# A planner whose segments end at dependences, a model of the shared port, and an opening with other orders and engines

## The chip, the cores and the metric

The kernel runs on one core of one Trainium2 chip. The metric is the device time of one execution in microseconds (us). The kernel before took 988.6 us, the median of three runs (987.35 to 989.39). The core's engines are TensorE (PE, with its weight loads apart as PEld), VectorE (DVE), ScalarE (ACT), GpSimd (POOL) and SyncE (SP), which issues every DMA of this kernel. Each engine works through its own list of instructions in the order in which they were emitted. Where one needs what another has written, it waits on a semaphore.

## The reference

Eight batches of attention with eight heads of 64: 32 global queries see all 544 keys, and 512 local queries see the 32 global keys and the keys at most 32 positions away. The 4352 rows that come out go through an MLP of 512, 2048 and 512 columns.

```python
def attention(q_l, k_l, v_l, q_g, k_g, v_g):          # B, H, S, D = 8, 8, 512 (32 global), 64
    k_all = np.concatenate([k_g, k_l], axis=2); v_all = np.concatenate([v_g, v_l], axis=2)
    out_g = sm(scale * q_g @ k_all.T) @ v_all
    s_ll = np.where(np.abs(pos[:, None] - pos[None, :]) <= 32, scale * q_l @ k_l.T, -1e9)
    out_l = sm(np.concatenate([scale * q_l @ k_g.T, s_ll], -1)) @ v_all
    return np.concatenate([out_g, out_l], axis=2)
def mlp(x, w_in, w_out):                              # 4352 x 512, 512 x 2048, 2048 x 512
    h = x @ w_in
    g = np.where(h >= 1, h, np.where(h <= -1, 0, (h + 1) ** 2 / 4))
    return g @ w_out
```

The softmax `sm` subtracts the row's maximum and divides by the sum. The two weight matrices come as 64-bit floats.

## The kernel before

**What is computed where.** Every product runs on TensorE in 16-bit halves: a number is a high and a low part, and three products of parts stand for one. So every operand is prepared first. ACT casts the high part, and DVE or POOL subtracts it to get the low part. The weights come as pairs of 32-bit words. `decode` puts the words of one tile of 128 x 512 together (ACT takes the magnitude, DVE shifts the low word and joins the two), `signed` sets the sign, TensorE sums the magnitudes for a scale, and `halves` scales and splits the tile; its three letters say on which engines (first `e`: on TensorE, with a float32 product by `const_sid`). There are 16 tiles of w_in (steps Lw, wd, ws, wh: load, decode, scale, halves) and 16 of w_out (Lo, od, oh).

**Attention.** K, Q and V of a batch are loaded, scaled and split (steps L, sk/sq/sv, pk/pq/pv), and K and Q are transposed. Step aa takes two heads of 128 queries: scores in `ps_s`, minimum and mask on DVE into `tts_t` and `small_nb`, a small DVE addition on `small_nb`, two exponentials on ACT into `pf_pf`, the high part into `const_pb`, the low part by POOL, and the transposed weights in `pt_pt`. Step ab multiplies these by V into `ps_x`, and step ax divides (`xn_xn`), splits (`xn_xh`) and transposes into `xt_xt` by a DMA. In batch 0 `turn` (lines 562 to 571) makes the transposes with eight matmuls by `const_ident` into PSUM and an ACT copy; in the other batches SP issues a transposing DMA.

**The MLP.** A stage is 256 rows, half a batch. Step m (`moe1`) makes two tiles of the hidden layer from `xt_xt` in 24 matmuls into `ps_h` and applies the activation on ACT, DVE, DVE, ACT and POOL (`moe_t_r`, `hidden_g`); step o (`moe2`) multiplies by w_out into `ps_o`. Step m2.0 is the first of the third stage, the second batch's first, and needs step ax11, the last of that half batch. There are 16 stages and two for the global rows.

**What sets the order.** The kernel is traced once into a list of calls. `segments` (line 152) groups successive calls of one step on one engine into a Segment, whose calls stay together; a call that reads what the call before it wrote adds 100 ns to the Segment's price. `schedule` (line 204) replays the Segments: on each engine the ready one with the smallest `prio` goes next. `prio` comes from the numbers in `T` (a nominal time of every step), then from `deadlines`, which counts back from the end. `plan` (line 310) does both, keeps the better, and `build` emits the calls in that order, so the order on every engine is fixed. Loads are paced: one is issued when the fifth before it has landed.

Until about 250 us the core prepares the weights, the first two batches and runs the first two stages; that part is called the opening here.

## Time and profile before

| what | value |
|---|---|
| median of the runs | 988.6 us |
| the profiled execution's own time | 987.26 us |
| its span, first to last instruction | 985.5 us |
| mean granted clock of TensorE | 0.968 |
| PE busy | 904.5 us, 92% |
| DVE busy | 730.4 us, 74% |
| ACT busy | 601.0 us, 61% |
| POOL busy | 359.5 us, 36% |

All times of rows are microseconds from the start of the span. A busy PE is not PE at its peak, since its records overlap. An instruction's duration is that from its start to its end; where two on one engine stand closer than the first one's duration, they overlap. What an engine waited for is inferred from semaphores. All instructions of the kernel before carry line 1238 (loads 1240), since they are emitted there; they are told apart by tiles, with buffer numbers left out.

### The profile page before, as it was taken

To read this page: it belongs to the slowest core of one execution; us is meant where nothing else is said; L and a number is where in the kernel's file an instruction comes from. 1 tells how busy PE (TensorE), PEld (TensorE's weight loads), DVE (VectorE), ACT (ScalarE), POOL (GpSimd) and SP (SyncE) were. 2 spreads that over 40 slices of the span, in tenths; PEclk is the share of its full clock that TensorE was granted. 3 is DMA by queue.
4 is the path that set the end of the run, shared out by engine and by line. 5 is a ranking of instruction groups with operands and counts; after the bars stand their busy time and mean duration, and the time that the engine had idled before them with its cause. 6 is when DMAs were issued, how large, how long until landed. Compare 5 with 4: busy or idle time off the path is not lost.

```text
span 985.5 us, 24720 instructions
## 1 busy us (share of the span) xinstructions
PE 904.5 (92%) x9499; PEld 641.4 (65%) x9500; DVE 730.4 (74%) x1956; ACT 601.0 (61%) x1418; POOL 359.5 (36%) x383
## 2 busy tenths in 40 slices
...
GB/s 236 233 147 64 168 88 102 145 161 144 175 155 177 119 128 152 182 113 128 153 186 45 134 111 170 136 114 130 160 175 114 128 134 108 59 79 66 33 1 33
DMA packets 370102, 125.23 MB, mean 127 GB/s; under 512 B 346432, under 2 KB 355648, under 8 KB 369984
## 3 DMA queue, kind: packets, MB, share of 16 engines
...
## 4 chain that ended last, share of the span: by engine, by line
PE 71%; DVE 16%; DMA 5%; issue 3%; ACT 2%; POOL 1%; SPq 1%; DVEq 0%; POOLq 0%; ACTq 0%
PE ps_h_h L1238 32%; PE ps_o_o L1238 30%; PE ps_s_s L1238 5%; PE ps_x_x L1238 5%; DVE tmp_tmp L1238 2%; DVE weights_w L1238 2%; DVE tts_t L1238 1%; DVE nat_nat L1238 1%; DMA xt_xt<-xn_xh 1%; DMA weights_w<-in_moe_w_in_dram 1%; DVE batch_small_ms L1238 1%; DVE ps_h_h L1238 1%; SPq L1238 1%; DVE moe_t_r L1238 1%; DVE batch_small_q L1238 1%
## 5 line engine op out<-in xcount | busy, mean ns | idle before, releaser
L1238 PE MATMUL ps_h_h<-xt_xt,weights_w 128*128 128x256 f16 (+1 forms) x3456 | 383.3, 270 | 10.2 <-ACT pt_pt L1238 6.0
L1238 PE MATMUL ps_o_o<-weights_w,hidden_g 128*128 128x512 f16 x1632 | 376.6, 381 | 2.8 <-DVE xt_xt L1238 2.8
L1238 PEld LDWEIGHTS <-weights_w 128*128 128x128 f16 x3456 | 321.7, 99 | 61.5 <-issue 15.5
L1238 PEld LDWEIGHTS <-hidden_g 128*128 128x128 f16 x1744 | 161.5, 100 | 177.6 <-issue 12.1
L1238 POOL TENSOR_TENSOR hidden_g<-moe_t_r,hidden_g 128x512 f16<-128x512 f32 (+1 forms) x144 | 165.6, 1150 | 273.2 <-ACT hidden_g L1238 267.2
L1238 POOL TENSOR_TENSOR const_pb<-pf_pf,const_pb 128x384 f16<-128x384 f32 (+1 forms) x124 | 129.3, 1045 | 276.9 <-DVE const_pb L1238 195.8
L1238 ACT ACTIVATE moe_t_r<-ps_h_h,batch_small_ms 128x512 f32<-128x512 f32 (+1 forms) x144 | 107.9, 749 | 127.2 <-PE ps_h_h L1238 119.3
L1238 DVE SCALAR_TENSOR_TENSOR ps_h_h<-ps_h_h,batch_small_ms,moe_t_r 128x512 f32<-128x512 f32 (+1 forms) x144 | 104.2, 723 | 93.0 <-ACT moe_t_r L1238 92.9
L1238 ACT ACTIVATE pf_pf<-tts_t,small_nb 128x224 f32<-128x224 f32 (+1 forms) x256 | 117.3, 459 | 91.2 <-DVE small_nb L1238 77.1
L1238 DVE CUSTOM_DVE_ANT_0 tts_t<-ps_s_s,const_mask,batch_small_q 128x192 f32<-128x192 f32 (+1 forms) x256 | 100.2, 427 | 41.1 <-PE ps_s_s L1238 39.0
L1238 ACT CAST hidden_g<-moe_t_r 128x512 f16<-128x512 f32 (+1 forms) x144 | 84.7, 588 | 61.0 <-DVE moe_t_r L1238 60.6
L1238 DVE SCALAR_TENSOR_TENSOR moe_t_r<-moe_t_r,batch_small_ms,ps_h_h 128x512 f32<-128x512 f32 (+1 forms) x144 | 103.4, 718 | 5.5
L1238 ACT ACTIVATE junk_junk<-stage_st 128x512 f16<-128x512 f32 (+1 forms) x108 | 67.5, 625 | 25.5 <-DMA stage_st<-in_v_l_dram 8.7
L1238 PE MATMUL ps_s_s<-kt_kt,qt_qa 128*128 128x32 f16 (+2 forms) x704 | 69.8, 199 | 10.4 <-DVE small_nb L1238 5.6
L1238 PEld LDWEIGHTS <-pt_pt 128*128 128x128 f16 (+1 forms) x1536 | 61.8, 98 | 15.4 <-ACT pt_pt L1238 2.5
L1238 PE MATMUL ps_x_x<-v_v,pt_pt 128*128 128x64 f16 (+1 forms) x1536 | 67.7, 194 | 0.8 <-DVE moe_t_r L1238 0.5
L1238 PE MATMUL ps_s_s<-kt_kt,qt_qb 128*128 128x32 f16 (+2 forms) x704 | 65.9, 198 | 0.0
L1238 PEld LDWEIGHTS <-qt_qb 128*128 128x128 f16 x704 | 55.4, 98 | 16.1 <-issue 13.1
L1238 PEld LDWEIGHTS <-qt_qa 128*128 128x128 f16 x704 | 59.4, 98 | 5.1 <-issue 1.5
L1238 DVE CAST const_pb<-pf_pf 128x384 f16<-128x384 f32 (+1 forms) x112 | 47.7, 431 | 10.7 <-DMA pt_pt<-const_pb 6.6
L1238 ACT ACTIVATION_READ_ACCUMULATOR pf_pf<-tts_t,small_nb 128x1 f32 x256 | 47.8, 187 | 0.0
L1238 DVE TENSOR_SCALAR small_nb<-small_nb 128x2 f32<-128x2 f32 x128 | 35.4, 277 | 4.4
(165 smaller groups left out, 900.5 us busy)
## 6 DMA issues: line engine op xcount, KB each, us to landing
...
```

What stands on the lines that cost most here:

```text
L1238: getattr(getattr(tc.nc, engine), op)(*a, **k)
```

## The change

The planner changes in four places. A Segment on DVE or ACT now ends where the next call reads what the call before it wrote, and calls of other steps may stand between the two. `shares` says which calls of DVE and POOL use a port that the two have in common, and `schedule` runs such calls one after the other (`pair`). `plan` makes one pass with `deadlines` and adds a number per step from a table, `LATER` (316 entries, in us). The prices of some calls and transfers are others.

The choice of engine moves into strings in `T`, read by `of`: `turns` (batch 0's 16 `pt_pt` are now DMA transposes, its ten K and Q ones stay), `casts` and `subs` (high and low part of `const_pb`), `glow`, `lows`, `splits`, `shifts` (six of 32 on POOL), `mags` and `halves`. `decode` can also take the magnitude on POOL. `win_scale` joins eight one-column maxima into three wider ones. In `T` the first tiles of w_in are loaded ahead of K and Q, and V much later.

```diff
+def shares(engine, op, a, k, tiles):
+    if engine == "gpsimd":
+        return op != "memset"
+    if engine != "vector" or op in ("memset", "reciprocal", "tensor_reduce", "tensor_tensor_reduce"):
+        return False
...
+    held = [x for x in ins if is_ap(x) and not tiles.get(x.tensor.name, (0, 0, 1))[2]]
+    return len(held) > 1 or (op in ("tensor_scalar", "tensor_copy") and len(held) == 1 and free(held[0]) > 1)
...
-            if cur is None or cur.engine != engine or engine == "sync" or fresh & {tiles[nm][0] for nm in cur.new}:
+            near = [x.tensor.name for x in sides(*cur.calls[-1])[0]] if cur and cur.engine == engine in ("vector", "scalar") else []
+            if (cur is None or cur.engine != engine or engine == "sync" or fresh & {tiles[nm][0] for nm in cur.new}
+                    or any(x.tensor.name in near for x in ins)):
                 cur = Segment()
...
-            near = [x.tensor.name for x in sides(*cur.calls[-2])[0]] if len(cur.calls) > 1 else []
-            cur.t += t + (100.0 if engine in ("vector", "scalar") and any(x.tensor.name in near for x in ins) else 0.0)
+            cur.t += t
+            cur.parts.append((t, shares(engine, op, a, k, tiles)))
...
+                done, slow = now, SLOW if e == "tensor" and now < 2.0e5 else 1.0
+                for t, shared in g.parts:
+                    if shared:
+                        pair = done = max(pair - LEAD, done) + t
+                    else:
+                        done += t * slow
...
-    for n in range(PASSES):
-        order, taken, end = schedule(segs, tiles, hop, slack, landing, ahead)
...
+    if T["late"]:
+        deadlines(segs, [g.n for g in segs], hop, slack, landing)
+    for g in segs:
+        g.prio += LATER.get(g.step, 0.0) * (1.0e3 if T["late"] else 1.0)
+    order, taken, _ = schedule(segs, tiles, hop, slack, landing, ahead)
...
-            for c in (n - 1, n):
-                nc.vector.tensor_max(W["tmh"][:, c:c + 1], wt[:, n - 1:n], wt[:, n:n + 1])
+            nc.vector.tensor_max(W["tmh"][:, n - 1:n + 1], wt[:, n - 1:n].broadcast_to([P, 2]), wt[:, n:n + 1].broadcast_to([P, 2]))
...
-        (nc.vector.tensor_copy if b else nc.scalar.copy)(pb[:, 0, :, :w], pf[:, :, :w])
-        nc.gpsimd.tensor_tensor(pb[:, 1, :, :w], pf[:, :, :w], pb[:, 0, :, :w], op=ALU.subtract)
+        (nc.scalar.copy if of("casts", b, 4 * i + pr, 16, "v") == "a" else nc.vector.tensor_copy)(pb[:, 0, :, :w], pf[:, :, :w])
+        (nc.vector if of("subs", b, 4 * i + pr, 16, "p") == "v" else nc.gpsimd).tensor_tensor(pb[:, 1, :, :w], pf[:, :, :w], pb[:, 0, :, :w], op=ALU.subtract)
...
-        turn(b, pt.rearrange("p j u c k -> p (j u c) k"), pb.rearrange("p j u c -> p (j u c)"))
+        turn(of("turns", b, 10 + 4 * i + pr, 30, "d"), pt.rearrange("p j u c k -> p (j u c) k"), pb.rearrange("p j u c -> p (j u c)"))
...
-T = dict(att=1.25, s0=72.5, s1=139.1, s2=221.06, wd0=8.61, wds=3.39, wd8=36.0, wdt=2.27, wh=1.5, whs=2.09, od=58.0, ods=2.6,
+T = dict(late=1, lk0=4.19, lq0=1.76, lv0=30, sk=12, sq=14, adds="vvvvvv1vvvvvvvvvvvvvavvvvvvvvv1v",
+         subs="pppppppppppvvvpppppppvpvvpppppvp", glow="pppppppppppvpppv",
...
```

The first place is the end of the first half tile of attention, on DVE. Before, it read as follows (the last call of one w_in tile's decode, then ax00, then the scales ms00; `DVE_49` is DVE's own semaphore):

```order
L1238 SCALAR_TENSOR_TENSOR tmp_tmp_3_120<-tmp_tmp_3_120,weights_w12_0_77 128x512 [waits DVE_49,Activation_49]
L1238 SCALAR_TENSOR_TENSOR weights_w12_0_77<-weights_w12_0_77,tmp_tmp_3_120 128x512 [waits DVE_49]
L1238 TENSOR_SCALAR small_den_0_161<-small_sum_0_138 128x8
L1238 RECIPROCAL small_rc_0_162<-small_den_0_161 128x8 [waits DVE_49]
L1238 TENSOR_TENSOR xn_xn_0_163<-ps_x_x_0_155,small_rc_0_162 128x512 [waits DVE_49,PE_49]
L1238 TENSOR_SCALAR batch_small_ms_0_170<-const_tm_0_131,batch_small_sv_0_123 128x2
L1238 TENSOR_SCALAR batch_small_ms_0_170<-batch_small_ms_0_170 128x2 [waits DVE_49]
L1238 RECIPROCAL batch_small_ms_0_170<-batch_small_ms_0_170 128x2 [waits DVE_49]
L1238 TENSOR_SCALAR batch_small_ms_0_170<-batch_small_ms_0_170 128x2 [waits DVE_49] x2
L1238 TENSOR_TENSOR batch_small_ms_0_170<-batch_small_ms_0_170 128x2 [waits DVE_49]
L1238 TENSOR_SCALAR batch_small_ms_0_170<-batch_small_ms_0_170 128x2 [waits DVE_49]
L1238 SCALAR_TENSOR_TENSOR batch_small_ms_0_170<-const_wt_0_81,batch_small_sv_0_123,batch_small_ms_0_170 128x2
```

Now the same two steps stand between others, and a w_out tile's decode (`stage_st_1`) is spread among them:

```order
L1280 TENSOR_SCALAR small_den_0_162<-small_sum_0_130 128x8
L1280 TENSOR_SCALAR stage_st_1_92<-stage_st_1_92 128x512 [waits DMAHW6_49,DMAHW5_49]
L1280 RECIPROCAL small_rc_0_163<-small_den_0_162 128x8 [waits DVE_49]
L1280 TENSOR_SCALAR batch_small_q5_0_113<-batch_small_q5_0_113,batch_small_sk_0_107 128x3
L1280 SCALAR_TENSOR_TENSOR tmp_tmp_1_87<-tmp_tmp_1_87,stage_st_1_92 128x512 [waits DVE_49,Activation_49]
L1280 TENSOR_TENSOR xn_xn_0_164<-ps_x_x_0_160,small_rc_0_163 128x512 [waits DVE_49,PE_49]
L1280 TENSOR_SCALAR batch_small_q5_0_113<-batch_small_q5_0_113 128x3 [waits DVE_49]
L1280 SCALAR_TENSOR_TENSOR weights_w0_0_66<-stage_st_1_92,tmp_tmp_1_87 128x512 [waits DVE_49]
L1280 TENSOR_SCALAR batch_small_ms_0_171<-batch_small_ms_0_171 128x2
L1280 TENSOR_SCALAR batch_small_ms_0_171<-const_tm_0_101,batch_small_sv_0_148 128x2
L1280 TENSOR_TENSOR const_tm_0_101<-const_tm_0_101 128x4
L1280 TENSOR_TENSOR batch_small_ms_0_171<-batch_small_ms_0_171 128x2 [waits DVE_49]
```

In this piece no row reads what the row ahead of it wrote. Counted over DVE's instructions up to the last of ax11, 231 of 471 waited for the very instruction ahead of them before, and 30 of 462 do now; 74 more wait for the one two ahead, where three did.

The second place is DVE's start. Before, its first rows were K's scale (`small_amk`, from ACT's squares) and Q's:

```order
L1238 MEMSET const_ones_0_82 128x128
L1238 TENSOR_REDUCE small_amk_0_91<-small_amk_0_91 128x1
L1238 TENSOR_SCALAR small_asx_0_93<-small_amk_0_91 128x1
L1238 COPY small_amk_0_91<-ps_s_s_0_97 128x1
L1238 TENSOR_SCALAR small_amk_0_91<-small_amk_0_91 128x1 x2
L1238 TENSOR_SCALAR batch_small_sk_0_98<-small_amk_0_91 128x1
L1238 RECIPROCAL batch_small_sk_0_98<-batch_small_sk_0_98 128x1
```

Now the first rows decode w_in tiles whose low words POOL has shifted:

```order
L1280 MEMSET const_ones_0_83 128x128
L1280 SCALAR_TENSOR_TENSOR tmp_tmp_0_96<-tmp_tmp_0_96,weights_w2_0_68 128x512
L1280 SCALAR_TENSOR_TENSOR tmp_tmp_1_87<-tmp_tmp_1_87,weights_w0_0_66 128x512
L1280 SCALAR_TENSOR_TENSOR tmp_tmp_2_95<-tmp_tmp_2_95,weights_w1_0_67 128x512
L1280 TENSOR_SCALAR weights_w3_0_69<-weights_w3_0_69 128x512
L1280 SCALAR_TENSOR_TENSOR weights_w1_0_67<-weights_w1_0_67,tmp_tmp_2_95 128x512
L1280 SCALAR_TENSOR_TENSOR tmp_tmp_3_97<-tmp_tmp_3_97,weights_w3_0_69 128x512
```

Tiles 2, 0 and 1 come first, two of DVE's calls for each, and K's scale comes after the fourth tile.

The third place is SP's queue in the middle of the opening, where before it held w_out's loads, copies of V and Q, and the first transposes into `xt_xt`:

```order
L1240 DMA stage_st_1_86<-in_moe_w_out_dram 128x512 x2
L1240 DMA stage_st_3_116<-in_moe_w_out_dram 128x512
L1238 DMA v2_v2_0_127<-v_v_3_126 64x1024
L1238 DMA qt_qb_2_157<-qt_qa_2_156 64x1024
L1240 DMA stage_st_3_116<-in_moe_w_out_dram 128x512
L1238 DMA qt_qb_2_157<-qt_qa_2_156 64x1024
L1238 DMA v2_v2_1_133<-v_v_5_132 64x1024
L1238 DMA_TRANSPOSE xt_xt_0_89<-xn_xh_0_164 128x8x128
L1238 DMA qt_qb_0_106<-qt_qa_0_104 64x1024 x2
L1238 DMA qg_qgb_0_166<-qg_qga_0_165 64x256 x2
L1240 DMA stage_st4_0_87<-in_k_l_dram 32x8x64
L1238 DMA_TRANSPOSE xt_xt_0_89<-xn_xh_0_164 128x8x128
```

Now the first `pt_pt` transposes stand there:

```order
L1282 DMA stage_st_0_93<-in_moe_w_out_dram 128x512 x2
L1280 DMA_TRANSPOSE pt_pt_0_134<-const_pb0_0_61 128x8x128
L1280 DMA_TRANSPOSE pt_pt_1_138<-const_pb1_0_62 128x8x128
L1280 DMA_TRANSPOSE pt_pt_2_145<-hidden_g_0_132 128x8x128
L1280 DMA v2_v2_0_156<-v_v_1_153 32x1024
L1280 DMA v2_v2_1_158<-v_v_1_153 32x1024
L1280 DMA v_v_0_159<-v_v_1_153 32x1024
L1280 DMA_TRANSPOSE pt_pt_0_134<-hidden_g_1_133 128x8x128
L1280 DMA v2_v2_0_156<-v_v_3_155 64x1024
L1280 DMA v2_v2_1_158<-v_v_5_157 64x1024
L1282 DMA stage_st_3_126<-in_moe_w_out_dram 128x512 x2
L1280 DMA_TRANSPOSE pt_pt_1_138<-const_pb0_0_61 128x8x128
```

All 16 of them go through SP, between the loads of w_out.

## Rows read from the trace of the kernel before

**Rows 1.** Windows: stretch, length, then busy us (instructions) per engine, clock, DMA share, GB/s.
```profile
0.00:253.00 253.00, 179.10 (x1791) 121.25 (x1793) 209.52 (x547) 186.32 (x412) 102.61 (x125) 0.88 0.64 149
253.00:985.50 732.50, 725.39 (x7709) 520.14 (x7707) 520.89 (x1410) 414.73 (x1006) 256.88 (x258) 1.00 0.64 119
...
0.00:248.00 248.00, 176.87 (x1753) 119.12 (x1755) 206.10 (x532) 182.48 (x399) 100.50 (x122) 0.89 0.63 149
```

**Rows 2.** Timeline of all engines, 244 to 254: start, us, instruction.
```profile
246.10 0.60 ACT L1238 CAST xn_xh<-xn_xn 128x512 f16<-128x512 f32 x1
...
246.23 0.17 DVE L1238 TENSOR_SCALAR small_nb<-small_nb 128x2 f32<-128x2 f32 x1
...
247.34 0.68 DVE L1238 TENSOR_TENSOR xn_xh<-xn_xn,xn_xh 128x512 f16<-128x512 f32 x1
...
249.51 1.30 SPq L1238 DMA_TRANSPOSE xt_xt<-xn_xh  x1
...
251.56 2.63 SPq L1238 DMA_TRANSPOSE pt_pt<-const_pb  x2
...
252.86 1.35 PE L1238 MATMUL ps_h_h<-xt_xt,weights_w 128*128 128x256 f16 x6 [0.58 <-DMA xt_xt<-xn_xh]
```

**Rows 3.** Timeline of DVE, first 13 us.
```profile
11.95 0.16 DVE L1238 TENSOR_REDUCE small_amk<-small_amk 128x1 f32<-128x5 f32 x1 [10.88 <-ACT junk_junk L1238]
```

**Rows 4.** Timeline of ACT, first 13 us.
```profile
7.91 0.20 ACT L1238 ACTIVATE const_warm<-const_pgb 128x1 f32<-128x1 f16 x1 [5.83 <-POOL small_amg L1238]
```

**Rows 5.** Groups of POOL, 0 to 248: busy us, mean ns of one, idle before.
```profile
L1238 POOL TENSOR_SCALAR tmp_tmp<-weights_w,const_wo 128x512 f32<-128x512 f32 x8 | 5.7, 722 | 4.0 <-DVE const_wo L1238 3.8
```

**Rows 6.** Groups of DVE, 0 to 248, same columns.
```profile
L1238 DVE SCALAR_TENSOR_TENSOR weights_w<-weights_w,tmp_tmp 128x512 int32<-128x512 int32 x15 | 13.8, 920 | 0.5
...
L1238 DVE SCALAR_TENSOR_TENSOR tmp_tmp<-tmp_tmp,stage_st 128x512 int32<-128x512 int32 x16 | 12.6, 788 | 2.3 <-ACT tmp_tmp L1238 0.7
L1238 DVE SCALAR_TENSOR_TENSOR weights_w<-stage_st,tmp_tmp 128x512 int32<-128x512 int32 x16 | 12.5, 782 | 0.6
...
L1238 DVE TENSOR_SCALAR small_nb<-small_nb 128x2 f32<-128x2 f32 x30 | 8.5, 284 | 1.0
...
L1238 DVE TENSOR_TENSOR weights_w<-tmp_tmp,weights_w 128x512 f16<-128x512 f32 x5 | 4.1, 826 | 0.0
L1238 DVE TENSOR_SCALAR batch_small_ms<-batch_small_ms 128x2 f32<-128x2 f32 x10 | 4.0, 400 | 0.3
```

**Rows 7.** Timeline of DVE near 28 and 95.
```profile
28.04 0.15 DVE L1238 TENSOR_SCALAR small_w<-small_w 128x1 f32<-128x1 f32 x1
28.23 0.16 DVE L1238 RECIPROCAL small_w<-small_w 128x1 f32<-128x1 f32 x1
28.31 0.13 DVE L1238 TENSOR_SCALAR small_w<-small_w 128x1 f32<-128x1 f32 x1
...
94.83 1.46 DVE L1238 SCALAR_TENSOR_TENSOR tmp_tmp<-tmp_tmp,stage_st 128x512 int32<-128x512 int32 x1
...
97.47 0.69 DVE L1238 SCALAR_TENSOR_TENSOR tmp_tmp<-tmp_tmp,stage_st 128x512 int32<-128x512 int32 x1
98.19 0.69 DVE L1238 SCALAR_TENSOR_TENSOR weights_w<-stage_st,tmp_tmp 128x512 int32<-128x512 int32 x1
98.80 0.41 DVE L1238 CUSTOM_DVE_ANT_0 tts_t<-ps_s_s,const_mask,batch_small_q 128x192 f32<-128x192 f32 x1
```

**Rows 8.** Timeline of POOL near 93.
```profile
93.22 2.53 POOL L1238 TENSOR_TENSOR weights_w<-tmp_tmp,weights_w 128x512 f16<-128x512 f32 x2
```

**Rows 9.** Groups: the first batch's transposes on PE, and ACT's moves.
```profile
L1238 PE MATMUL ps_h_h<-const_ident,const_pb 128*128 128x128 f16 x96 | 8.6, 229 | 8.9 <-DVE moe_t_r L1238 3.4 <-POOL const_pb L1238 2.4 <-ACT const_pb L1238 1.2
...
L1238 ACT COPY pt_pt<-ps_h_h 128x1024 f16<-128x1024 f16 x16 | 16.0, 1002 | 0.3 <-PE ps_h_h L1238 0.2
```

**Rows 10.** Waits of PE, 0 to 250: engine, tile, releaser: us, times, longest.
```profile
PE ps_h_h L1238 <- ACT pt_pt L1238: 8.2, 7, 2.2
```

**Rows 11.** DMA issues, 0 to 250: count, median us from issue to landing.
```profile
pt_pt<-const_pb SPq DMA_TRANSPOSE x10, 3.3
```

More of the change, by code (lines that the diff above doesn't have):

```diff
@@ L129, in cost @@
         run = min(tuple(x.ap[-1])[1] * mybir.dt.size(x.dtype) for x in (o, ins[0]))
-        return 560.0, b / (186.0 if run < 512 else 264.0 if run < 1024 else 280.0)
+        return 560.0, b / (215.0 if run < 512 else 340.0)
     if engine == "scalar":
-        own = 90 if op != "activation" or mybir.dt.size(o.dtype) == 2 else 190 if "accum_out" in k else 235
+        ptr = any(free(x) == 1 for x in ins[1:])
+        if "accum_out" in k:
+            own = 190 if ptr else 95
+        elif mybir.dt.size(o.dtype) == 2:
+            own = 185 if ptr else 90
+        else:
+            own = 235 if ptr else 135
         return own + n / 1.2 + (93 if "accum_out" in k else 0), 0
@@ L148 @@
 class Segment:
-    __slots__ = ("n", "engine", "calls", "t", "xfer", "after", "before", "new", "uses", "load", "step", "left", "ready", "prio", "t0", "done")
+    __slots__ = ("n", "engine", "calls", "t", "xfer", "after", "before", "new", "uses", "load", "step", "parts", "left", "ready", "prio", "t0", "done")
 def segments(steps, tiles, prio, names):
@@ L221, in schedule @@
         if g.left == 0:
-            waiting[g.engine].append(g)
+            bisect.insort(waiting[g.engine], (g.prio, g.n, g))
     free_at = {e: 0.0 for e in engines}
-    dma_free, now, events, order, landed = 0.0, 0.0, [], [], []
+    dma_free, pair, now, events, order, landed = 0.0, 0.0, 0.0, [], [], []
     while len(order) < len(segs) or events:
@@ L232, in schedule @@
                 best = None
-                for g in waiting[e]:
-                    if g.ready > now or (best is not None and (g.prio, g.n) > (best.prio, best.n)):
+                for at, (_, _, g) in enumerate(waiting[e]):
+                    if g.ready > now:
                         continue
@@ L239, in schedule @@
                             need.setdefault(tiles[nm][0], []).append(place[nm])
-                    if any(len(slots[tag]) < len(x) + (min(x) > head[tag]) or max(x) - head[tag] >= many[tag] for tag, x in need.items()):
+                    if need and any(len(slots[tag]) < len(x) + (min(x) > head[tag]) or max(x) - head[tag] >= many[tag] for tag, x in need.items()):
                         continue
@@ L280, in schedule @@
                 c = segs[b]
-                wait = (hop if c.engine != g.engine else 60.0) + (slack if c.engine == "tensor" and g.engine != "tensor" else 0.0)
+                wait = (hop if c.engine != g.engine else OWN) + (slack if c.engine == "tensor" and g.engine != "tensor" else 0.0)
                 c.ready = max(c.ready, now + wait)
@@ L302, in deadlines @@
             c = segs[b]
-            wait = (hop if c.engine != g.engine else 60.0) + (slack if c.engine == "tensor" and g.engine != "tensor" else 0.0)
+            wait = (hop if c.engine != g.engine else OWN) + (slack if c.engine == "tensor" and g.engine != "tensor" else 0.0)
             x = min(x, late[b] - wait - took)
@@ L570, in turn, with of @@
             nc.tensor.transpose(t[:, c, :n], i[:, c * P:(c + 1) * P], ident[:n, :n])
-        nc.scalar.copy(o, t[:, :, :n])
+        (nc.scalar.copy if who == "a" else nc.vector.tensor_copy)(o, t[:, :, :n])
+    def of(what, b, n, most, other):
+        return T[what][most * b + n] if most * (b + 1) <= len(T[what]) else other
     def load_win(f):
@@ L630, in wout_decode @@
         raw = W.pop(("rawo", f))
-        m = decode(raw.rearrange("p c t -> p (c t)"), None, SHIFTS[NF + f])
+        m = decode(raw.rearrange("p c t -> p (c t)"), None, T["shifts"][NF + f], T["mags"][NF + f])
         mag = upper(m)
```

113 lines of the change are left out of this document (61 added, 52 removed), and 39 rows, old and new, of the table LATER.

## The prediction

> **What bounds the kernel now.** I read the windows first. From 253 us to the end PE is busy 725 of 732.5 us at a granted clock of 1.00, so that part is PE's own and ends when PE has done its matmuls. In the 253 us ahead of it PE is busy 179 us: some 74 us of PE are lost there, and almost nothing later [rows 1]. The cut is where the first matmul of the third stage, m2.0, starts, 252.9 us [rows 2]. So the time is the start of m2.0 plus what PE has left by then. Its work behind m2.0 is the same in both kernels to 0.3 us, by the sum of the matmuls' columns at 2.4 GHz that stand behind m2.0 in the two orders. The question is thus one number: when m2.0 can start.
>
> Then I followed m2.0 back in the timeline. It waits for the DMA transpose of `xn_xh`, which SP issued at 249.5, after DVE's subtraction of 247.3 to 248.0, the last call of ax11 on DVE [rows 2]. Up to there DVE is busy 206.1 of 248.0 us, ACT 182, PE 177 and POOL 100 [rows 1]; the engine that is nearest to full is DVE. Of its 41.9 idle us, 10.9 lie at the start, where its first real call waits for ACT's squares until 11.95 [rows 3]. The 31 that remain are many small pieces. So I treat the opening as DVE's, and forecast when DVE ends ax11.
>
> **The change part by part.** *The start.* DVE's first call is now the decode of w_in tile 2. It needs POOL's two shifts, which stand behind POOL's constants, and ACT's magnitude, which stands behind `const_warm`; that one starts at 7.91, as soon as POOL's memsets are through [rows 4]. Two POOL calls of 0.72 us by the nearest row [rows 5] after 7.9 it is about 9.4. DVE starts at 9.4 for 11.95: **-2.5 us**. The bounds are 0, if a load of w_in is late, and -3.5, if the shift is not waited for.
>
> *DVE's load.* Up to ax11 DVE has 462 calls for 471. Eight low parts (six of `const_pb`, two of `hidden_g`) come from POOL to DVE, at some 0.7 to 0.83 us by the nearest row, that of `weights_w` [rows 6]; six shifts, five column maxima, two casts and some single calls go. With each group's own mean, from the view whose dearest groups are [rows 6], that is 10.1 us less and 7.3 more: **-2.8 us**. The bounds are -4 (nine calls at the mean of 206.1/471) and +3 (nothing saved but the added low parts stretched).
>
> *Self-waits.* Of those calls 231 waited for the call right ahead, and 30 do now. The price of one such wait stands in the timeline: the second of two dependent calls starts 0.72 us after the first (97.47 to 98.19), an independent one of the same kind is followed after 0.61 (98.19 to 98.80); of small calls the dependent one starts after 0.19 (28.04 to 28.23), the independent one after 0.08 [rows 7]. Both differ by 0.11 us. So 201 fewer give **-22.1 us**. The cover is gone only where the call put between waits for another engine itself, since DVE takes its calls in order; bounded by 0 and -22. The 74 that wait for the call two ahead cost little, as a call of 0.08 or more lies between.
>
> *The shared port.* A DVE call of 0.69 us took 1.46 (94.83), while a POOL subtraction ran beside it [rows 7, 8]. Over the opening such stretching can be read from the means: 15 calls of 0.92, 16 of 0.79 and 16 of 0.78 where the undisturbed one takes 0.69, thirty of 0.28 where one takes 0.17 [rows 2, 6, 7], and ten of 0.40 of that same kind: 3.4 + 1.6 + 1.5 + 3.4 + 2.3 = 12.2 us. The replay now runs such pairs one after the other and so sees them, and eight of POOL's subtractions go. I take **-10 us**, near that end, since a few long collisions make up most of the excess. The bounds are -12 and, if the new order puts more of DVE's calls beside POOL's, +12.
>
> *The last step.* The subtraction of ax11 is POOL's now, some 1.2 us (2.53 for two [rows 8]) for 0.68: **+0.5**. The rest of the way to m2.0, 4.8 us from 248.0 [rows 2], stays.
>
> *PE and ACT.* 128 transposes leave PE and 16 copies of 1.0 us leave ACT [rows 9]; PE's waits for those copies, 8.2 us [rows 10], go with them. I cost this at nothing, since both engines have room beside DVE. One tile more is split on PE, also under that cover. SP gets 16 transposes of about 1.3 us each (2.63 for two in the later batch), and each lands 3.3 us after its issue [rows 2, 11], against some 2 us by PE and ACT (eight short matmuls and a copy of 1.0). That is 21 us of SP over some 100 us, between loads that are issued ahead; I cost it at nothing and keep the other case as a rival.
>
> *DVE's other waits.* The 31 us of small pieces hold the self-waits' gaps too. I take no change for the rest; the bounds are -16 (half of them) and +20.
>
> The sum: 248.0 - 2.5 - 2.8 - 22.1 - 10 = 210.6 us for DVE; + 4.8 + 0.5 = 215.9 for m2.0, where it was 252.9. That is 37.0 us less, a span of 985.5 - 37.0 = 948.5. The profiled execution's own time is 1.8 above its span (987.3), and the median of the runs is 1.3 above that: 951.6, so **952 us**.
>
> **The rivals.**
>
> *DVE's own pipe sets the spacing, not the semaphore.* Then parting dependent calls gives nothing, and the term of 22.1 falls away: 974 us. For it: the intervals compared differ in what comes second, a subtraction-like call or one that reads PSUM. Against it: large and small calls show the same 0.11 [rows 7]. The Trainium skill, VectorE: DVE Perf Modes, section The DRAIN you can't avoid, says that the next DVE call does not start until the pipe is empty and that a semaphore after each of eight copies cost nothing extra. By that rule the self-waits are free; the intervals of this trace, 0.72 and 0.61, disagree.
>
> *PE becomes the opening's bound.* PE is busy 179 of 253 us [rows 1] and works in order too. If its 74 idle us all stay, since each is the wait for some operand that the searched order delays elsewhere, only its work shrinks: 128 transposes at 8.6/96 us each [rows 9] (the records overlap, so the group's busy time counts), 11.5 us less. That gives 977 us. Against it: its clearest wait, for `pt_pt`, does vanish [rows 10].
>
> *The gain is larger.* The replay sees the waits as well; if the port's 12.2 go whole and half of DVE's 31 small idle us too, the time is 952 - 2 - 16 = 934. Against it: the replay is no chip, and an order fitted to it can miss.
>
> *Slower.* The 16 `pt_pt` transposes stand in SP's list between loads of w_out. SP takes its list in order, so a transpose that waits for POOL's low part holds back every load behind it, and the decode on DVE waits in turn. If each holds the list for its whole 3.3 us [rows 11], that is 53 us, 16 more than the 37 gained: 1004 us. It decides from 37/16 = 2.3 us each. For it: before, no transpose of batch 0's first half tiles went through SP, and its list was free for loads. Against it: loads are issued well ahead and DVE has other decodes to go on with.
>
> **How the numbers follow.** The forecast has 0.58, with a range of its own of 942 to 963 (the port's -12 and some waits below, half of the self-waits above); DVE's pipe 0.12, PE 0.14, larger 0.08, slower 0.08. The range of 930 to 977 holds the forecast, the larger gain and the pipe's case, and leaves out half of PE's case, which may come out on either side of its price, and the slower one. A measurement can tell 0.2%, about 2 us. All cases but the last lie well under 986.6. PE's case reaches it if PE's waits also grow by 10 us. So faster has 0.89, no change 0.04, slower 0.07.
>
> **What would show it.** In the profile after: m2.0 near 216 us and PE busy nearly without a gap behind it, in about 732 us; DVE's first decode near 9.4; DVE busy near 170 to 180 us up to ax11; thirty-odd `small_nb` additions with a mean near 0.19 and joining calls near 0.7; independent neighbours on DVE 0.61 apart. The forecast is wrong if DVE's idle time up to ax11 grows beyond the 31 us by much, with SP's transposes or PE as what it waits for; if the mean of independent calls does not fall; or if PE shows new gaps after m2.0, where I count on none.

## The result: 974.4 us, 14 of the 37 us that were forecast

The changed kernel takes 974.4 us (median of 4 runs, 973.9 to 976.9) for 988.65 before (median of 4): 0.9862 of it, 95% interval 0.9843 to 0.9882. The direction was right. The time lies inside the wide range, but only because that range was drawn to hold the pipe's case as well; 952 was forecast: 37 us were to go, 14 went. In the profiled execution (974.65 us, span 972.9 for 985.5) it is 12.6.

**The cut at m2.0.** The windows of the changed kernel's span, with the columns of [rows 1]: the part ahead of m2.0, the part behind it, and the part up to DVE's end of ax11.

```profile
0.00:234.60 234.60, 166.47 (x1666) 112.04 (x1667) 188.05 (x541) 167.28 (x389) 118.38 (x131) 0.88 0.82 177
234.60:972.90 738.30, 727.53 (x7709) 521.65 (x7708) 508.48 (x1411) 415.00 (x1016) 256.50 (x259) 0.99 0.66 119
...
0.00:229.20 229.20, 163.64 (x1617) 109.30 (x1617) 183.73 (x523) 164.65 (x382) 116.19 (x129) 0.89 0.81 178
```

m2.0 starts at 234.6 for 252.9, where 215.9 was forecast; so 18.3 us were won up to there. Behind it the kernel takes 738.3 us for 732.6 (985.5 - 252.9), so 5.7 are given back there, with PE busy 727.5 in place of 725.4 and a clock of 0.99 in place of 1.00.

**DVE's road to ax11.** It ends at 229.2 for 248.0. I took it apart by adding over the records of DVE's calls up to ax11: their durations, less the time in which a call overlaps the one ahead, plus idle time in pieces under 0.2 us and in longer ones. Calls of one kind have the same operation, tiles and shape; what a call takes beyond the shortest sixth of its kind counts as stretched.

| up to ax11, us | before | after | difference | forecast |
|---|---|---|---|---|
| durations, part that is stretched | 31.9 | 26.0 | -5.9 | -10 |
| durations, the rest | 192.3 | 189.2 | -3.1 | -2.8 |
| overlap with the call ahead (taken off) | 18.1 | 31.5 | -13.4 | |
| idle pieces under 0.2 us | 10.7 | 1.7 | -9.0 | |
| these two together: self-waits | | | -22.4 | -22.1 |
| longer waits at the start | 10.9 | 14.8 | +3.9 | -2.5 |
| longer waits elsewhere | 20.3 | 28.9 | +8.6 | 0 |
| end of ax11 | 248.0 | 229.1 | -18.9 | -37.4 |

Busy time (durations less overlap) and short pieces together fell by 31.4 us, from 216.8 to 185.4; the longer waits took 12.5 back, and 18.9 arrived.

What the parting of calls does shows well where ax00 ends; the timeline of DVE there (start, us, instruction):

```profile
75.46 0.16 DVE L1280 TENSOR_SCALAR small_den<-small_sum 128x8 f32<-128x8 f32 x1
75.54 0.41 DVE L1280 TENSOR_SCALAR stage_st<-stage_st 128x512 int32<-128x512 int32 x1
75.87 0.19 DVE L1280 RECIPROCAL small_rc<-small_den 128x8 f32<-128x8 f32 x1
75.98 0.17 DVE L1280 TENSOR_SCALAR batch_small_q<-batch_small_q,batch_small_sk 128x3 f32<-128x3 f32 x1
76.07 0.68 DVE L1280 SCALAR_TENSOR_TENSOR tmp_tmp<-tmp_tmp,stage_st 128x512 int32<-128x512 int32 x1
76.67 0.68 DVE L1280 TENSOR_TENSOR xn_xn<-ps_x_x,small_rc 128x512 f32<-128x512 f32 x1
77.27 0.16 DVE L1280 TENSOR_SCALAR batch_small_q<-batch_small_q 128x3 f32<-128x3 f32 x1
77.34 0.68 DVE L1280 SCALAR_TENSOR_TENSOR weights_w<-stage_st,tmp_tmp 128x512 int32<-128x512 int32 x1
77.94 0.16 DVE L1280 TENSOR_SCALAR batch_small_ms<-batch_small_ms 128x2 f32<-128x2 f32 x1
```

These calls stand without a gap: the next one starts 0.60 us behind a call of 0.68, 0.33 behind the one of 0.41 and 0.07 to 0.11 behind a short one; before, dependent ones were 0.72 and 0.19 apart [rows 7].

**The port.** The groups that answer to [rows 6]:

```profile
L1280 DVE SCALAR_TENSOR_TENSOR tmp_tmp<-tmp_tmp,stage_st 128x512 int32<-128x512 int32 x16 | 14.9, 931 | 2.5 <-ACT tmp_tmp L1280 2.4
L1280 DVE SCALAR_TENSOR_TENSOR weights_w<-stage_st,tmp_tmp 128x512 int32<-128x512 int32 x16 | 13.5, 853 | 0.0
...
L1280 DVE SCALAR_TENSOR_TENSOR weights_w<-weights_w,tmp_tmp 128x512 int32<-128x512 int32 x15 | 11.1, 756 | 0.0
...
L1280 DVE TENSOR_SCALAR small_nb<-small_nb 128x2 f32<-128x2 f32 x27 | 5.6, 213 | 0.0
...
L1280 DVE TENSOR_SCALAR batch_small_ms<-batch_small_ms 128x2 f32<-128x2 f32 x10 | 4.6, 460 | 0.0
```

Two groups are much better (0.92 to 0.76 and 0.28 to 0.21), two are worse (0.79 to 0.93, 0.78 to 0.85), and the scales `batch_small_ms` still take 0.46 for 0.17. Added up as the prediction did it, the excess of these five groups is 11.6 us for 12.2: in the place where I had looked for the 10 us, 0.6 went. The 5.9 of the table are over all kinds of calls. The stretching moved more than it went away.

**The start.** The timeline of POOL, whose first six shift calls are one entry:

```profile
7.97 9.25 POOL L1280 TENSOR_SCALAR weights_w<-weights_w 128x512 f32<-128x512 uint16 x6
```

The timeline of DVE, its first three decodes:

```profile
10.70 0.69 DVE L1280 SCALAR_TENSOR_TENSOR tmp_tmp<-tmp_tmp,weights_w 128x512 int32<-128x512 int32 x1 [9.64 <-POOL weights_w L1280]
13.98 0.69 DVE L1280 SCALAR_TENSOR_TENSOR tmp_tmp<-tmp_tmp,weights_w 128x512 int32<-128x512 int32 x1 [2.58 <-POOL weights_w L1280]
17.26 0.69 DVE L1280 SCALAR_TENSOR_TENSOR tmp_tmp<-tmp_tmp,weights_w 128x512 int32<-128x512 int32 x1 [2.59 <-POOL weights_w L1280]
```

The groups of POOL's calls (busy us, mean ns of one, idle us just before):

```profile
L1280 POOL TENSOR_SCALAR weights_w<-weights_w 128x512 int32<-128x512 f32 x5 | 10.2, 2044 | 0.4
...
L1280 POOL TENSOR_SCALAR weights_w<-weights_w 128x512 f32<-128x512 uint16 x5 | 4.7, 935 | 0.4
```

DVE's first three decodes wait 9.6, 2.6 and 2.6 us for POOL. Each shift is two calls, 0.94 and 2.04 us; the three take 9.25, and DVE gets going at 17.3, not at 9.4 [rows 3, 4]. My 0.72 was that of a call which multiplies f32 by a scale [rows 5]; the call that writes int32 from f32 costs almost three times that. I had also counted the wait for the first tile alone. At 1.44 us a tile DVE, which needs 0.70 for each of its calls here, would still have stood some 0.7 twice more; by that estimate 1.5 of the 6.4 us between -2.5 and +3.9 come from there and the rest from the price.

**The waits elsewhere.** The waits of DVE up to 229 us (us in total, times, longest):

```profile
DVE tmp_tmp L1280 <- POOL weights_w L1280: 14.8, 3, 9.6
DVE ps_h_h L1280 <- ACT moe_t_r L1280: 8.1, 4, 3.5
...
DVE const_pb L1280 <- DMA pt_pt<-const_pb: 2.2, 2, 1.7
```

The line of the kernel before, up to 248 us:

```profile
DVE ps_h_h L1238 <- ACT moe_t_r L1238: 2.9, 2, 2.5
```

`ps_h_h` waited 2.9 us for ACT before and 8.1 now. The longest one, in DVE's timeline:

```profile
205.49 0.76 DVE L1280 SCALAR_TENSOR_TENSOR ps_h_h<-ps_h_h,batch_small_ms,moe_t_r 128x512 f32<-128x512 f32 x1 [3.46 <-ACT moe_t_r L1280]
```

What ACT did ahead of it, in ACT's timeline:

```profile
203.74 0.51 ACT L1280 CAST const_pb<-pf_pf 128x384 f16<-128x384 f32 x1 [2.16 <-DMA pt_pt<-const_pb]
204.16 0.61 ACT L1280 CAST hidden_g<-moe_t_r 128x512 f16<-128x512 f32 x1
204.68 0.77 ACT L1280 ACTIVATE moe_t_r<-ps_h_h,batch_small_ms 128x512 f32<-128x512 f32 x1
```

DVE waits for m1.12's activation (204.68), and ACT, which takes its list in order, had stood 2.2 us at a cast into `const_pb` until a DMA transpose had emptied that buffer. DVE's own waits for such a buffer are 2.2 us more. The other longer waits have many releasers, and I did not follow them back.

**Behind m2.0.** A line of PE's waits from 240 us to the end (us in total, times, longest):

```profile
PE ps_x_x L1280 <- DMA pt_pt<-const_pb: 4.0, 4, 2.2
```

The place of the longest one, in PE's timeline:

```profile
298.12 0.53 PE L1280 MATMUL ps_x_x<-v_v,pt_pt 128*128 128x64 f16 x12 [2.17 <-DMA pt_pt<-const_pb]
...
299.70 3.95 PE L1280 MATMUL ps_o_o<-weights_w,hidden_g 128*128 128x512 f16 x12
```

An o-group at full clock, and the window behind the wait (its last three numbers are the granted clock, the DMA share and GB/s):

```profile
190.22 2.75 PE L1280 MATMUL ps_o_o<-weights_w,hidden_g 128*128 128x512 f16 x12
298.00:304.00 6.00, 5.88 (x53) 3.52 (x54) 4.21 (x13) 3.75 (x11) 2.62 (x4) 0.72 0.90 216
```

PE stands 2.17 us for a `pt_pt` DMA, and behind that the o-group at 299.7 takes 3.95 us for 2.75. The granted clock is 0.72 from 298 to 304 us: within it 0.50, the lower of the two levels (1.2 of 2.4 GHz), from 298.7 to 302.1.

**The last step.** DVE's `xn_xn` ends at 229.2; in the timeline, ACT's cast, POOL's subtraction, the transpose and m2.0 follow:

```profile
229.39 0.60 ACT L1280 CAST xn_xh<-xn_xn 128x512 f16<-128x512 f32 x1
...
230.07 1.15 POOL L1280 TENSOR_TENSOR xn_xh<-xn_xn,xn_xh 128x512 f16<-128x512 f32 x1 [1.66 <-DMA pt_pt<-const_pb]
...
231.25 1.23 SPq L1280 DMA_TRANSPOSE xt_xt<-xn_xh  x1
...
234.60 0.80 PE L1280 MATMUL ps_h_h<-xt_xt,weights_w 128*128 128x256 f16 x3 [0.52 <-DMA xt_xt<-xn_xh]
```

5.4 us, for 4.8 + 0.5 forecast.

### The profile page after: what moved, and what is told of

Its sections match the earlier page's. It is cut to its first block, busy times and chain, and to the rows that moved or that the text cites. A ratio compares the mean times of both kernels' runs of the same rounds, so it can differ in the third digit from the quotient of the medians.

```text
span 972.9 us, 24493 instructions
## 1 busy us (share of the span) xinstructions
PE 894.0 (92%) x9375; PEld 633.7 (65%) x9375; DVE 696.5 (72%) x1951; ACT 582.3 (60%) x1405; POOL 374.9 (39%) x390
## 4 chain that ended last, share of the span: by engine, by line
PE 67%; DMA 11%; DVE 8%; ACT 6%; issue 4%; POOL 2%; SPq 1%; ACTq 0%; DVEq 0%; POOLq 0%
PE ps_h_h L1280 30%; PE ps_o_o L1280 28%; PE ps_s_s L1280 5%; PE ps_x_x L1280 4%; DMA pt_pt<-const_pb 3%; DMA stage_st<-in_k_l_dram 2%; DMA qt_qa<-nat_nat 1%; ACT junk_junk L1280 1%; DMA stage_st<-in_moe_w_out_dram 1%; ACT pf_pf L1280 1%; DVE tts_t L1280 1%; DMA stage_st<-in_v_l_dram 1%; POOL const_pb L1280 1%; DVE tmp_tmp L1280 1%; DVE weights_w L1280 1%
## 5 line engine op out<-in xcount | busy, mean ns | idle before, releaser
L1280 PEld LDWEIGHTS <-hidden_g 128*128 128x128 f16 x1712 | 158.7, 98 | 183.2 <-issue 17.0
L1280 POOL TENSOR_TENSOR const_pb<-pf_pf,const_pb 128x384 f16<-128x384 f32 (+1 forms) x117 | 120.6, 1032 | 225.7 <-DVE const_pb L1280 89.4
L1280 ACT ACTIVATE pf_pf<-tts_t,small_nb 128x192 f32<-128x192 f32 (+1 forms) x256 | 117.0, 458 | 97.2 <-DVE small_nb L1280 77.3
L1280 DVE CAST const_pb<-pf_pf 128x384 f16<-128x384 f32 (+1 forms) x109 | 47.8, 440 | 41.0 <-ACT pf_pf L1280 23.0
L1280 PE MATMUL ps_s_s<-kt_kt,qt_qa 128*128 128x128 f16 (+2 forms) x704 | 69.3, 200 | 8.3 <-DVE small_nb L1280 5.7
L1280 PEld LDWEIGHTS <-pt_pt 128*128 128x128 f16 (+1 forms) x1536 | 61.8, 99 | 22.9 <-DMA pt_pt<-const_pb 10.9
L1280 PE MATMUL ps_s_s<-kt_kt,qt_qb 128*128 128x128 f16 (+2 forms) x704 | 65.8, 199 | 0.0
L1280 PE MATMUL ps_o_o<-tmp_tmp,const_ones 128*128 128x128 bf16 (+1 forms) x76 | 14.3, 311 | 23.5 <-DVE tmp_tmp L1280 23.4
## 6 DMA issues: line engine op xcount, KB each, us to landing
weights_w<-in_moe_w_in_dram SPq DMA_DIRECT2D x32, 256.0 KB, 4.1
stage_st<-in_q_l_dram SPq DMA_DIRECT2D x32, 256.0 KB, 4.2
stage_st<-in_moe_w_out_dram SPq DMA_DIRECT2D x32, 256.0 KB, 3.7
out_dram<-tmp_tmp SPq DMA_DIRECT2D x30, 256.0 KB, 2.6
stage_st<-in_k_l_dram SPq DMA_DIRECT2D x24, 256.0 KB, 3.8
stage_st<-in_v_l_dram SPq DMA_DIRECT2D x21, 256.0 KB, 4.4
```

Source lines behind the costliest of these rows:

```text
L1280: getattr(getattr(tc.nc, engine), op)(*a, **k)
```

## The experiments

Ten of the fourteen keep the changed kernel's plan and alter one thing in it ("plan kept"). m2.0 is where its first matmul starts in the profiled run; it is 234.6 in the changed kernel. Each ratio is to runs of the kernel before that were taken with that run, whose medians lie between 986.6 and 988.4 us; so medians of different rows can differ by some 2 us without a cause.

| run | median us | ratio to before (95%) | m2.0 |
|---|---|---|---|
| e1 self-waits put back | 993.3 | 1.0059 (1.0046 to 1.0071) | 249.9 |
| e2 three shifts on DVE | 970.5 | 0.9823 (0.9810 to 0.9837) | 233.1 |
| e3 the split alone, on before | 985.5 | 0.9971 (0.9962 to 0.9980) | 249.1 |
| e4 pt_pt on PE, planned anew | 990.6 | 1.0025 (1.0014 to 1.0035) | 256.0 |
| e5 more DVE work early | 979.2 | 0.9904 (0.9888 to 0.9921) | 241.5 |
| e6 more DVE work late | 976.5 | 0.9879 (0.9865 to 0.9894) | 239.0 |
| e7 o3.00 ahead of ab202 | 971.2 | 0.9828 (0.9813 to 0.9843) | 234.8 |
| e8 e2 and e7 | 968.55 | 0.9805 (0.9779 to 0.9831) | 232.9 |
| e9 port not seen, planned anew | 996.8 | 1.0102 (1.0070 to 1.0133) | 254.9 |
| e10 no table, planned anew | 980.6 | 0.9939 (0.9918 to 0.9960) | 248.7 |
| e11 all six shifts on DVE, e7 | 964.4 | 0.9774 (0.9751 to 0.9796) | 229.8 |
| e12 less PE work in m1 | 972.45 | 0.9849 (0.9825 to 0.9873) | 233.7 |
| e13 cast behind m1.12 | 975.0 | 0.9871 (0.9855 to 0.9887) | 236.3 |
| e14 e11 and e13 | 966.3 | 0.9788 (0.9774 to 0.9801) | 230.0 |

**e1: the price of a self-wait.** DVE's list is altered after planning: a call goes back behind the call of its step that it reads, where no other call is in the way.

```diff
+    order = regroup(order, segs, sketch.tiles, taken)
...
+    for q in [x for x in order if segs[x].engine == "vector"]:
...
+        p = [x for x in segs[q].after if segs[x].engine == "vector" and segs[x].step == segs[q].step]
...
+        if not any(clash(p, x) for x in order[i + 1:j]):
+            order.insert(j - 1, order.pop(i))
```

> The changed kernel with its plan kept; only DVE's list is altered: wherever nothing forbids it, a call that reads what the call of its own step wrote is put right behind it again. Up to ax11, 163 of 462 calls then wait for the very call ahead, for 30 in the changed kernel. Theory (the wait on DVE's own semaphore costs 0.11 us each): 133 x 0.11 = 14.6 us more on DVE up to ax11, m2.0 starts near 245 to 249 us for 234.6, and the median goes from 974.4 to 984 to 989. Rival (DVE's own pipe sets the spacing, the semaphore costs nothing): 972.5 to 976.5.

993.3 us: 18.9 slower than the changed kernel, and slower than before. In the same taking apart, ax11 ends at 244.7, 15.5 later; overlap and small gaps lose 13.8 us for 133 more self-waits, 0.104 each. The stretching grows by 9 us as well, and the long waits shrink by 9: a slower DVE finds more of its inputs ready. The place shown above, in DVE's timeline of e1:

```profile
79.81 0.22 DVE L1322 TENSOR_SCALAR batch_small_q<-batch_small_q,batch_small_sk 128x3 f32<-128x3 f32 x1
80.07 0.17 DVE L1322 TENSOR_SCALAR batch_small_q<-batch_small_q 128x3 f32<-128x3 f32 x1
80.15 0.68 DVE L1322 SCALAR_TENSOR_TENSOR tmp_tmp<-tmp_tmp,stage_st 128x512 int32<-128x512 int32 x1
80.86 0.69 DVE L1322 SCALAR_TENSOR_TENSOR weights_w<-stage_st,tmp_tmp 128x512 int32<-128x512 int32 x1
81.47 2.00 DVE L1322 TENSOR_SCALAR batch_small_ms<-batch_small_ms 128x2 f32<-128x2 f32 x2
```

0.71 us to the dependent call (80.15 to 80.86), 0.61 to the independent one behind it. So the rival by which parting dependent calls gives nothing is refuted; that its price, 974, was met has other reasons. The Trainium skill, VectorE: DVE Perf Modes, section The DRAIN you can't avoid, measured eight copies, where a semaphore after each cost nothing extra; that does not carry over to the calls of this kernel, where the wait costs 0.104 us.

**e2, e8, e11: the start.** Plan kept; the decode of w_in tiles 2, 0 and 1 (in e11 of all six tiles) shifts on DVE.

```diff
-        if who == "p":
+        if who == "x":
...
+            nc.vector.tensor_scalar(lo, lo, 29, None, op0=ALU.logical_shift_right)
+        elif who == "p":
...
+        T.update(shifts="xxx" + T["shifts"][3:])
```

> The changed kernel with its plan kept; only the low-word shifts of the first three w_in tiles (2, 0, 1) go from POOL (two calls of 1.54 us each) back to DVE (one of 0.42). Theory (POOL's shifts hold DVE's start): the first decode on DVE starts near 7 us for 10.7, the three are done by about 12 for 18, and as DVE bounds the opening m2.0 comes 4 to 6 us sooner: 968 to 971. Rival (the start is held by the loads and by ACT's wait for K, so nothing is won): 973 to 976.

DVE's timeline of e2, from its first call:

```profile
4.37 0.45 DVE L1286 TENSOR_SCALAR weights_w<-weights_w 128x512 int32<-128x512 int32 x1 [3.31 <-DMA weights_w<-in_moe_w_in_dram]
7.10 1.06 DVE L1286 TENSOR_SCALAR weights_w<-weights_w 128x512 int32<-128x512 int32 x1 [2.28 <-DMA weights_w<-in_moe_w_in_dram]
8.08 0.67 DVE L1286 SCALAR_TENSOR_TENSOR tmp_tmp<-tmp_tmp,weights_w 128x512 int32<-128x512 int32 x1
...
12.53 0.43 DVE L1286 TENSOR_SCALAR weights_w<-weights_w 128x512 int32<-128x512 int32 x1 [2.24 <-DMA weights_w<-in_moe_w_in_dram]
```

970.5, 3.9 us less. DVE begins at 4.4 and now waits for the loads, 3.3, 2.3 and 2.2 us. Of the 6 to 7 us that the start had cost against the forecast, m2.0 gets back only 1.5 and the end 3.9 (2.6 in the profiled execution, the slowest of the four). The start is real, but what follows takes part of it back. DVE's first call of K's scale, in the timelines of the changed kernel and of e2:

```profile
23.67 0.14 DVE L1280 TENSOR_REDUCE small_amk<-small_amk 128x1 f32<-128x5 f32 x1
...
19.62 0.16 DVE L1286 TENSOR_REDUCE small_amk<-small_amk 128x1 f32<-128x5 f32 x1 [2.61 <-ACT junk_junk L1286]
```

DVE, 4 us ahead there, now waits 2.6 for ACT's squares, as the rival had it in part; at 80 us the same calls stand only 1.6 us sooner than in the changed kernel.

**e7: behind m2.0.** Plan kept, PE's list alone: o3.00 stands ahead of ab202.

```diff
+    at = pe.index(next(n for n in pe if segs[n].step == "ab202"))
+    up = [n for n in pe[at:at + 12] if segs[n].step == "o3.00"]
...
+    order[at:at] = up
```

> The changed kernel with its plan kept, and on PE's list alone step o3.00 (12 matmuls) put ahead of ab202, which waits for a pt_pt DMA at 296 to 298 us. Theory (that wait and the low clock behind it are part of what is lost after m2.0): 2.2 us of wait and about 2 of low clock go, 970 to 973. Rival (the wait moves to the next step that needs a pt_pt): 973.5 to 976.

971.2, 3.3 us less, with m2.0 at 234.8 unmoved, and PE's waits on `pt_pt` behind 240 fall to 0.3 us by 320. The part behind m2.0 takes 734.6 us for 738.3, so 3.7 of the 5.7 us lost there are this one wait and the clock that fell behind it. At 320 us e7 is 4.1 us ahead; near 380 a wait for ACT (`xg_xgf`, 2.0 us for 1.6) has a lower clock behind it (0.91 from 370 to 390 us, 1.00 in the changed kernel) and takes part of that back.

e8 is e2 and e7 together.

> Both edits together: the three first shifts on DVE and o3.00 ahead of ab202. If they act in different places they add up: 970.5 less 2 to 4, so 966 to 969. If the gain of the first was the loss behind m2.0 in another form: 970 to 972.

968.55: 2.0 below e2, 2.6 below e7; its own runs spread over 6.5 us, so whether the two add up fully is not settled by the medians. In the profiled executions they do: the spans are 2.6, 3.4 and 6.1 us under the changed kernel's.

e11 is e7 with the six shifts that the plan had left to POOL on DVE:

```diff
+        T.update(shifts=T["shifts"].replace("p", "x"))
```

> The changed kernel with its plan kept, all six shifts that it gave to POOL back on DVE, and o3.00 ahead of ab202. Theory (a POOL shift of two calls of 1.5 us holds a DVE that could do it in 0.42): a little more than with the first three alone, 965 to 968.5. Rival (the later three were hidden): as with the first three, 967 to 970.

964.4 is the best of all, 10 us under the changed kernel and 4.1 under e8, which differs by the three later shifts alone. The two ratios' intervals overlap, but m2.0 too starts 3.1 us sooner than in e8: the later shifts were not hidden. m2.0 in PE's timeline of e11:

```profile
229.76 2.51 PE L1292 MATMUL ps_h_h<-xt_xt,weights_w 128*128 128x256 f16 x14 [0.35 <-DMA xt_xt<-xn_xh]
```

**e3, e10: the split without a fitted order.** e3 is the kernel before with the new end of Segments (and the 100 ns of a self-wait put between two Segments) and no other part; e10 the changed kernel with an empty table.

```diff
+            near = [x.tensor.name for x in sides(*cur.calls[-1])[0]] if cur and cur.engine == engine in ("vector", "scalar") else []
...
+                    or any(x.tensor.name in near for x in ins)):
```

> The kernel before with one part of the change alone: a Segment on DVE or ACT ends where the next call reads what the call before it wrote (own price 100 ns between the two); its numbers, engines, loads and two passes as before. 57 self-waits up to ax11 for 231. Theory (0.11 us each): 174 x 0.11 = 19 us less on DVE, of which two thirds arrive: 972 to 979. Rival 1 (pipe): 987 to 990. Rival 2 (the time is handed back as waits on other engines): 982 to 987.

985.5. The largest of DVE's waits in e3, up to 245 us:

```profile
DVE ps_h_h L1239 <- ACT moe_t_r L1239: 13.3, 6, 9.3
```

DVE's busy time up to ax11 falls from 206.1 to 192.4 and the short idle pieces from 10.7 to 3.0, but the long waits grow from 31.2 to 47.8, one of them 9.3 us on ACT for m1.0, and ax11 ends at 243.2. So 21.3 us are saved on DVE and 4.8 arrive: most of what the parting saves turns into waits.

```diff
-        g.prio += LATER.get(g.step, 0.0) * (1.0e3 if T["late"] else 1.0)
+        g.prio += 0.0
```

> The changed kernel planned anew with LATER left out: the order comes from the deadlines alone. Theory (the split gives DVE its 20 us, but an order not fitted to the waits hands them back, as in the kernel before with the split alone): 985 to 995. Rival (the rules are the gain and the table is not): 972 to 980.

980.6, just above the rival's range: without any table 6 us better than the kernel before beside it (986.6), and 6 to 8 worse than with the table. The stretching up to ax11 is 32.9 us here and the long waits 48.6. The model of the port is in force in e10, and the stretching is no less than the 31.9 before: by itself the model does not lower it.

**e4, e9: the DMA transposes and the model of the port.** Both are planned anew with a table that was fitted to the other plan, so they hold an unknown amount of misfit.

```diff
-         turns="aaaaaaaaaadddddddddddddddd...
+         turns="aaaaaaaaaaaaaaaaaaaaaaaaaa...
```

> The changed kernel with batch 0's 16 pt_pt transposes on PE and ACT again, and planned anew with the same table. Theory (the DMA transposes cost little; ACT's 16 copies of 1.0 us and 128 short matmuls come back, and the table no longer fits): 978 to 990. Rival (SP's list holds the transposes and their waits back, so PE and ACT do them sooner): 966 to 972.

990.6, just past the theory's range. Nothing here speaks for SP's transposes as a brake, but with the misfit in it the run does not rule them out.

```diff
-    if engine == "gpsimd":
-        return op != "memset"
+    return False
```

> The changed kernel planned anew with one line in front: shares() is always false, so the replay runs DVE's and POOL's calls beside each other at full speed; LATER and all else as they are. Theory (the model of the port is worth some 6 us of stretched calls in the opening): the stretch of DVE's calls up to ax11 goes from 25 back to 31 us or more, and the median rises to 980 to 988, part of it because LATER was fitted with the model. Rival (the model is worth nothing on the chip): 972 to 977.

996.8, beyond the range I gave. The stretching goes to 32.3 us as expected, 6.3 more, but ax11 ends 20 us later, with long waits of 54.2 us for 43.7. Most of this loss is then something else, by my reading the misfit of the table; and since e10 has as much stretching with the model in force, e9 does not show what the model is worth either.

**e5, e6, e12: what bounds 138 to 197 us?** PE is busy 57.1 of these 59 us, so I formed the theory that PE had become the bound there, and that DVE's savings fell into waits for it. e5 and e6 issue some of DVE's calls twice; of TWICE the line of e5 stands here, in e6 it names the calls of the steps pk1, pq1 and pv1.

```diff
+    return step in {f"od{f}" for f in range(12)} and op == "scalar_tensor_tensor" and a[2] == -0x80000000
...
-                        getattr(getattr(tc.nc, engine), op)(*a, **k)
+                        for _ in range(2 if engine == "vector" and TWICE(segs[n].step, op, a) else 1):
+                            getattr(getattr(tc.nc, engine), op)(*a, **k)
```

> The changed kernel with its plan kept and DVE's sign call of w_out tiles 0 to 11 issued twice (same inputs, same result): 12 calls of 0.69 us, 0.61 to 0.72 apart, between about 77 and 126 us, so 7.3 to 8.6 us more DVE work in the stretch before PE is full. Theory (DVE bounds the opening up to about 138 us, then PE does): nearly all of it arrives, 980 to 983 for 974.4. Rival (DVE bounds the opening all the way to ax11, as predicted): the same 980 to 983. Rival (neither; waits on other engines hide it): 974 to 977. Read with the next run.

> The changed kernel with its plan kept and DVE's low-part calls of the second batch's K, Q and V (10 calls of 0.75 us, about 155 to 195 us) issued twice: 6.5 to 7.5 us more DVE work in the stretch in which PE is busy without a gap. Theory (PE bounds 138 to 197 us, so DVE has room there): 974 to 977.5. Rival (DVE bounds the opening all the way to ax11, as predicted): 980 to 982.

e5: m2.0 6.9 us later, the median 4.8 (7.5 in the profiled execution, the slowest of the four). e6: the median only 2.0, in the theory's range; but m2.0 is 4.4 later, so more than half of the added work does arrive there and is made up behind it. So I took PE's work away instead:

```diff
+                    if engine == "tensor" and segs[n].step.startswith("m1.") and at % 12 in (2, 5, 8):
+                        continue
```

> The changed kernel with its plan kept; in the eight steps m1 (160 to 204 us) six of the 24 matmuls are left out (the product of w_in's high part with x's low part, three of four column blocks), so the hidden layer of rows 256 to 511 is less exact. 48 matmuls of 256 columns, 0.11 us each, 5.1 us of PE. Theory (PE bounds 138 to 197 us and DVE waits for it there): m2.0 starts 4 to 5 us sooner than 234.6 and the median is 969 to 971. Rival (DVE and the second batch's chain bound that stretch, PE is only just full): PE waits instead, m2.0 within 1.5 us of 234.6, 973 to 975.5.

m2.0 in PE's timeline of e12:

```profile
233.68 6.57 PE L1282 MATMUL ps_h_h<-xt_xt,weights_w 128*128 128x256 f16 x44 [0.35 <-DMA xt_xt<-xn_xh]
```

Two of PE's waits ahead of it (us in total, times, longest):

```profile
PE ps_s_s L1282 <- DVE small_nb L1282: 5.0, 4, 3.7
...
PE ps_h_h L1282 <- DVE moe_t_r L1282: 2.3, 2, 1.8
```

m2.0 moves by 0.9 us of 5.1: PE waits instead, for `small_nb` 5.0 us (3.5 in the changed kernel) and for `moe_t_r` 2.3 (0.5). The theory falls: PE is full there, but only just. The median, 972.45, spreads from 968.8 to 975.3 and settles nothing by itself. The profiled execution is the fastest of them, and it won its time behind m2.0 (733.4 us for 738.3), where PE's wait for `pt_pt` is 0.2 us for 2.2.

**e13, e14: the buffer.** ACT's cast of aa102 into `const_pb` goes behind m1.12's last activation.

```diff
+    late = [n for n in act if segs[n].step == "aa102" and segs[n].calls[0][0] == "copy"]
...
+    at = order.index(last) + 1
+    order[at:at] = late
```

> The changed kernel with its plan kept; on ACT's list alone the cast of aa102 into const_pb, which waits for a pt_pt DMA transpose to free the buffer, stands behind m1.10's cast and m1.12's activation. Theory (ACT's list, held by a DMA transpose, holds DVE): DVE's wait of 3.5 us at 205 falls to about 1.3, m2.0 starts 1 to 2.5 us sooner than 234.6, median 972 to 974. Rival (the wait moves to the next call that needs the buffer): m2.0 within 0.7 us of 234.6, 974 to 976.

Two of DVE's waits in e13, from 138 to 235 us:

```profile
DVE const_pb L1290 <- DMA pt_pt<-const_pb: 5.3, 3, 2.5
DVE ps_h_h L1290 <- ACT moe_t_r L1290: 4.8, 3, 2.2
```

975.0, no gain. DVE's waits for ACT in 138 to 235 fall from 7.2 to 4.8 us, those for a `const_pb` buffer rise from 2.2 to 5.3: the wait moved to the next call that needs one of the two buffers. m2.0 is 1.7 us later than in the changed kernel, but this execution was 1.0 late already at 195 us, ahead of the moved cast.

e14 is e11 and e13 together.

> All six shifts on DVE, o3.00 ahead of ab202, and the cast of aa102 behind m1.12's activation. If the third repair adds: 962 to 963.5, for 964.4 with the first two. If its wait only moves: 964 to 966.

966.3, not below e11.

## Why the prediction was wrong

The forecast had the cut and the largest term right, and the bound as far as it was tested: DVE's extra calls move m2.0 (e5, e6), PE's missing ones hardly do (e12). ACT and POOL, for which DVE waits, were not tested in this way. The self-waits gave 22.4 us for 22.1, at 0.104 to 0.11 each, by the trace and by e1. DVE's load gave 3.1 for 2.8, the last step 0.6 for 0.5.

The step that failed is "DVE's other waits ... I take no change for the rest". They grew by 8.6 us up to ax11, inside the bound of +20 that I had set and given no weight. A saved microsecond of an engine with 83% of the span is not a microsecond of the end: once DVE's calls come closer together, its in-order list arrives sooner at calls whose inputs are not ready, and they stand there. e3 is the pure case: 21.3 us of DVE's time saved, 4.8 arriving; e1 is the reverse, where a slower DVE stood 9 us less. In the changed kernel, with 31.4 saved and 18.9 arriving, the one place followed back is the second batch's attention, where a step needs one of two `const_pb` buffers and a DMA transpose to free it. e13 shows that this wait does not go away when one call is moved. Whether a third buffer would free it was not tried, and for the other waits the releasers stay open.

Three terms were mis-sized. The start was +3.9 for -2.5, since the shifts cost 2.98 us a tile on POOL and not 1.44 (e2, e11), and three tiles in a row wait for them, not one. The port was -5.9 for -10, and -0.6 in the five groups that the 10 were read from: it is in the replay, but the calls that are stretched became others. And "PE has left by then" was 738.3 for 732.6: I had counted on no new gap, and one wait with the low clock behind it made 3.7 of the 5.7 (e7). Together: 8.6 + 6.4 + 4.1 + 5.7 = 24.8, less some 0.5 by which self-waits and load beat the forecast, for the 24.4 us between 37.0 and 12.6.

Of the rivals, 974 was the price of DVE's own pipe, which e1 refutes; that a rival names the right time is no evidence for its mechanism. "PE becomes the bound", at 977, came nearly as close. It had right that PE's idle time ahead of m2.0 would mostly stay (68.1 us for 73.9); but PE is not what holds that part (e12). The larger gain and the slower case did not come. What 16 transposes more in SP's list cost is not settled: e4 holds the misfit, and in the trace a `pt_pt` transpose up to m2.0 lands after 3.9 us, for 3.3 before.
